# Block transposes on VectorE with a trip through DRAM in place of TensorE's transposes, in a fused attention and two-MLP kernel

## The chip, the cores and the metric
The program runs on one core of a Trainium2 chip, in one launch. The metric is the device time of that core in microseconds. A core has five engines with a queue each: TensorE (PE in the profile; its weight loads are PEld), VectorE (DVE), ScalarE (ACT), GpSimd (POOL) and SyncE (SP). An engine works through its own queue in order; semaphores make it wait for others. All transfers of this kernel but the instruction fetches are issued on SP's queue.

## The reference
Sliding-window attention (4 batches, 8 heads, 576 positions, head size 64, window 64), whose output is reshaped to 2304 tokens of 512 and goes through two MLPs:

```
scores = scale * q @ k.T ; mask 0 <= i - j < 64 ; softmax ; @ v        # per head
h = x @ w_in (512 -> 2048) ; g = h * tanh(softplus(h)) ; x2 = g @ w_out (2048 -> 512)
h = x2 @ w_in2 (512 -> 1024) ; solu = h * softmax(h)
ln = (solu - mean) / sqrt(var + 1e-6) * g_ln ; out = ln @ w_out2 (1024 -> 512)
```

## The kernel before, in words
Matmuls run in a 32-bit form with each operand split in a high and a low part (`hi`, `lo`), three products per pair of operands where both are split.

**Attention.** The tokens come in 36 blocks of 64 queries. The first four blocks are done singly, the other 32 in 16 pairs n = 4, 6, ... 34 (`attend`). A pair goes: scores into PSUM (`a_qk`), from pair 8 on scaling and mask on VectorE into an SBUF tile `s` (`a_scale`), maximum, subtraction, exponential, sum, reciprocal, multiplication, then eight 128x128 transposes on TensorE into PSUM (`a_tr`, L837), two copies back to SBUF on ScalarE (`a_pt`), and the second product with v (`a_pv`, L874), whose result is split into the token tile `xt` of its group. There are five groups of tokens (512, 512, 512, 384, 384).

**First MLP.** 84 items (`mish`), each a group of tokens by 128 of the 2048 hidden units: first layer (`pe_m1`, L920, 12 matmuls), activation on ScalarE, split, second layer (`pe_m2`, L954, 8 matmuls, `pe_m2l`, L965, 4) into four PSUM accumulators, evicted and stored to DRAM (`x2d`).

**Second MLP.** 18 tiles of 128 tokens, two at a time (u = 0 to 8). Two tiles are loaded, combined to sums, split; seven products of half-size blocks (`b_p`, L1089, six matmuls each) go to four PSUM banks, are evicted and added on VectorE (`b_c`). Per tile: maximum, exponential, product and moments, normalisation in place in tile `h_b` (`b_z`, L1165), eight 128x128 transposes on TensorE into PSUM (`b_tr`, L1172), split by ScalarE (`b_hi`, L1178) and VectorE (`b_lo`, L1182), output matmuls (`b_m4`, L1197, three groups of eight), eviction on ScalarE (`b_out`, L1204) and store (L1208).

**What sets the order.** A planner (`Schedule`) walks all steps, with a cost per engine and buffer rings of given sizes, and issues the step that can start first by its costs; among near ones the table `RANK`, one number per step, decides. What each engine runs, and in which order, is thus fixed before the program runs. Waits come from data and buffers. Where the planner sees TensorE idle, it fills in matmuls on zeros (`bridge`, L687).

Of the kernel before, what the change touches and what calls it, by code (L numbers as in the profile page):

```python
# [1615 lines left out]
```

## Time and profile before

| | us |
|---|---|
| device time, median of 3 runs | 684.72 (683.97 to 684.91) |
| the profiled execution | 684.38 |
| its span | 682.5 |
| TensorE busy | 672.4 (99%) |
| VectorE busy | 393.7 (58%) |
| ScalarE busy | 346.5 (51%) |
| GpSimd busy | 37.4 (5%) |

The span runs from the first to the last instruction; the execution's own time holds a little more. Busy times count the time in which an engine runs something. The chain of waits follows back from the last instruction, at each step to what released it or to the instruction ahead of it on its engine, and so says what a shorter piece would be worth.

### The profile page before, as it was taken

What the parts mean: (1) busy time and instruction counts of PE and PEld (TensorE: products, weight loads), DVE (VectorE), ACT (ScalarE), POOL (GpSimd) and SP (SyncE); (2) the same over time, 40 slices, a digit from 0 to 9 for tenths busy, and PEclk for the clock granted to TensorE, in tenths of its full rate; (3) what the DMA queues carried; (4) which work ended last, traced back from release to release, by engine and by line L of the source; (5) the groups of instructions that cost most, each with busy time, mean ns of one, the idle gap of its engine ahead of it and who ended that gap; (6) DMA issues with size and microseconds to landing.
All of it is one profiled execution on the core that took longest, in us unless ns stands there. A gap on an engine that the chain in (4) does not pass through costs nothing.

```text
span 682.5 us, 10711 instructions
## 1 busy us (share of the span) xinstructions
PE 672.4 (99%) x4326; PEld 581.2 (85%) x4326; DVE 393.7 (58%) x693; ACT 346.5 (51%) x623; POOL 37.4 (5%) x63
## 2 busy tenths in 40 slices
PE   8899999999999999999999999999999999999997
PEld 6788888888888888888899999999888888888886
DVE  4887887775676143111116637747686678484461
ACT  6889965443357243112223545547665455564352
POOL 3212100000001000000001000000010001000010
PEclk9999999999999999999999999999999999999999
DMA  9886575563355020000043235103310111010001
GB/s 325 323 278 215 164 242 161 179 215 123 120 179 198 0 92 33 0 1 0 11 145 124 63 124 181 52 27 98 109 42 36 63 47 46 32 48 31 16 31 47
DMA packets 36801, 72.00 MB, mean 105 GB/s; under 512 B 2832, under 2 KB 14096, under 8 KB 36752
## 3 DMA queue, kind: packets, MB, share of 16 engines
q1 hardware_dynamic: 36752, 71.32, 31.0%
q8 instruction: 34, 0.56, 0.3%
q14 instruction: 15, 0.12, 0.1%
HBM read 59.77 MB, written 11.53 MB: 104 GB/s over the span
## 4 chain that ended last, share of the span: by engine, by line
PE 95%; DMA 2%; ACT 1%; issue 0%; DVE 0%; SPq 0%; ACTq 0%
PE ps_h L920 29%; PE x L954 19%; PE po L1197 14%; PE pb L1089 13%; PE x L965 10%; PE ps_o L874 2%; PE ps_s L735 2%; PE pt L1172 2%; PE ps_t L837 2%; DMA st<-w_out 1%; DMA qk<-qk 1%; PE ps_s L717 0%; ACT st L473 0%; PE ps_h L687 0%; ACT L930 0%
## 5 line engine op out<-in xcount | busy, mean ns | idle before, releaser
L920 PE MATMUL ps_h<-xt,w 128*128 128x512 f32 (+2 forms) x1008 | 205.3, 360 | 0.2 <-ACT mc L930 0.2
L920 PEld LDWEIGHTS ps_h<-xt,w 128*128 128x128 f32 x1008 | 177.0, 188 | 21.8 <-ACT mc L930 0.6
L954 PE MATMUL x<-g,w 128*128 128x512 f32 (+2 forms) x672 | 146.9, 360 | 0.5 <-DVE g L409 0.5
L954 PEld LDWEIGHTS x<-g,w 128*128 128x128 f32 x672 | 118.4, 188 | 14.9 <-DVE g L409 0.8
L425 DVE SCALAR_TENSOR_TENSOR g<-mc,g 128x512 fp32r<-128x512 f32 (+2 forms) x84 | 51.0, 613 | 94.5 <-ACT g L405 93.8
L1197 PE MATMUL po<-w,lz 128*128 128x512 f32 x432 | 102.4, 391 | 0.0
L930 ACT ACTIVATE mc<-ps_h 128x512 f32<-128x512 f32 (+2 forms) x84 | 44.4, 535 | 99.7 <-PE ps_h L920 84.7
L1197 PEld LDWEIGHTS po<-w,lz 128*128 128x128 f32 x432 | 80.7, 188 | 16.8
L965 PE MATMUL x<-g,w 128*128 128x512 f32 (+2 forms) x336 | 80.5, 361 | 0.0
L965 PEld LDWEIGHTS x<-g,w 128*128 128x128 f32 x336 | 59.6, 188 | 7.2 <-issue 0.7
L405 ACT ACTIVATE g<-mc 128x512 fp32r<-128x512 f32 (+2 forms) x59 | 33.8, 575 | 61.7 <-PE x L965 60.9
L1089 PE MATMUL pb<-w,xs 128*128 128x512 f32 x210 | 52.2, 398 | 0.0
L1089 PEld LDWEIGHTS pb<-w,xs 128*128 128x128 f32 x210 | 38.9, 188 | 8.7
L1182 DVE TENSOR_TENSOR lz<-pt,lz 128x512 fp32r<-128x512 f32 x36 | 24.0, 687 | 30.7 <-ACT lz L1178 30.6
L1089 PE MATMUL pb<-w,xs_w 128*128 128x512 f32 x168 | 40.8, 393 | 0.0
L1089 PEld LDWEIGHTS pb<-w,xs_w 128*128 128x128 f32 x168 | 31.2, 188 | 6.4
L409 DVE CAST g<-mc 128x512 fp32r<-128x512 f32 (+2 forms) x25 | 9.9, 395 | 43.4 <-PE x L965 41.3
L825 POOL TENSOR_TENSOR s<-s,rs 128x1024 f32<-128x1024 f32 x7 | 15.1, 2157 | 337.5 <-DVE rs L819 336.2
L490 DVE SCALAR_TENSOR_TENSOR st<-st 128x1024 uint32<-128x1024 uint32 x22 | 27.4, 1248 | 8.8 <-ACT st L482 6.2
L417 ACT ACTIVATE s<-ps_t 128x512 f32<-128x512 f32 x32 | 18.1, 596 | 25.3 <-PE ps_t L837 25.3
L1204 ACT ACTIVATE o<-po 128x512 f32<-128x512 f32 x18 | 10.8, 599 | 38.5 <-PE po L1197 37.7
L482 ACT ACTIVATE st<-st 128x1024 uint32<-128x1024 uint32 x22 | 25.1, 1147 | 9.8 <-DMA st<-w_in 4.2
(138 smaller groups left out, 757.1 us busy)
## 6 DMA issues: line engine op xcount, KB each, us to landing
qk<-qk SPq DMA_DIRECT2D x32, 512.0 KB, 5.2
st<-w_out SPq DMA_DIRECT2D x12, 1024.0 KB, 5.1
st<-w_in SPq DMA_DIRECT2D x10, 1024.0 KB, 5.9
v<-v SPq DMA_DIRECT2D x32, 256.0 KB, 3.8
xr<-x2d SPq DMA_DIRECT2D x18, 256.0 KB, 3.3
out<-o SPq DMA_DIRECT2D x18, 256.0 KB, 2.0
x2d<-xs SPq DMA_DIRECT2D x12, 256.0 KB, 2.7
part<-xs SPq DMA_DIRECT2D x8, 256.0 KB, 4.8
```

What stands on the lines that cost most here:

```text
L405: nc.scalar.activation(out=hi, in_=x, func=ACTF.Copy, scale=1.0 if g is None else g)
L417: nc.scalar.activation(out=out, in_=x, func=ACTF.Copy)
L425: nc.vector.scalar_tensor_tensor(out=lo, in0=x, scalar=1.0 if g is None else g, in1=hi.bitcast(F32), op0=ALU.mult, op1=ALU.subtract)
L482: nc.scalar.activation(out=w, in_=w, func=ACTF.Copy, scale=0.9325 * 2.0**-29)
L490: nc.vector.scalar_tensor_tensor(out=lw, in0=uw, scalar=3, in1=lw, op0=ALU.logical_shift_left, op1=ALU.bitwise_or)
L920: nc.tensor.matmul(out=ps[:, :n], lhsT=w[:, a, k, fs], rhs=x[:, b, k, a0:a1], start=(idx == 0), stop=(idx == len(terms) - 1),)
L930: nc.scalar.activation(out=c[:, :n], in_=ht.pop(i)[:, :n], func=ACTF.Mish)
L954: nc.tensor.matmul(out=acc[j][m][:, a0:a1], lhsT=w[:, a, f % 4, m * P:(m + 1) * P], rhs=g[:, 0, :n], start=(i in opens and a == 0), stop=F ...
L965: nc.tensor.matmul(out=acc[j][m][:, a0:a1], lhsT=w[:, 0, f % 4, m * P:(m + 1) * P], rhs=g[:, 1, :n], start=False, stop=i in closes,)
L1089: nc.tensor.matmul(out=ps, lhsT=x[:, a, ix, k, :], rhs=w[:, k, :], start=first and n == 0, stop=n == len(terms) - 1, skip_group_check=not ...
L1182: nc.vector.tensor_tensor(out=lt[t][:, 1, fs], in0=pst[t][:, fs], in1=lt[t][:, 0, fs].bitcast(F32), op=ALU.subtract)
L1197: nc.tensor.matmul(out=po[t], lhsT=lz[:, a, f, :], rhs=wt["w4", f // 4][:, b, f % 4, :], start=(c == 0 and idx == 0), stop=(c == 2 and idx ...
```

## The change
The transposes of the pairs n >= 16 (ten pairs) and of all 18 tiles of the second MLP leave TensorE. For those pairs the score tile `s` is laid out in four column blocks of 32, so that scaling is four instructions; one VectorE instruction (`nc.vector.transpose`) transposes each 32x32 block, one DMA writes the tile to DRAM (`blocks_out`, 512 KB) and four DMAs read it back (`blocks_in`, 128 KB each, to 32 partitions, in pieces of 1 KB), which puts the blocks in their places. In the second MLP it is the same, from `h_b` into a tile `y_b`, and back into `h_b`, which the split then reads. The ring of `h_b` grows from 4 to 6; the PSUM pool for the transposes goes. The warm-up at the start has 16 matmuls of one kind instead of 13 of another and 5 of it. `RANK` holds new numbers, so the order changes everywhere. The diff, cut to its core:

```
+N_T = 16
+SPLIT = "p f (i c) -> p i f c"
...
+    def blocks_out(key, src):
+        d = blocks[key] = dram.tile([4, 32, 4, 256], F32, tag="t_d", name="t_d", bufs=4)
+        nc.sync.dma_start(out=d.rearrange("i a b x -> (i a) b x"), in_=src.rearrange("p b h c -> p b (h c)"))
+
+    def blocks_in(key, dst):
+        d = blocks.pop(key)
+        for b in range(4):
+            r = slice(32 * b, 32 * b + 32)
+            nc.sync.dma_start(out=dst[r].rearrange("a i h c -> a i (h c)"), in_=d[:, :, b].rearrange("i a x -> a i x"))
...
-        z = m_p.tile([P, 2, GMAX], F32R, tag="g", name="warm_r", bufs=LAG)
...
-        zeros(a, 5)
+        zeros(ps_h.tile([P, 512], F32, tag="h", name="ps_w"), N_WARM)
...
+            s = at_p.tile([P, 4, 2 * NP, 32], F32, tag="s2", name="s", bufs=2)
+            for b in range(4):
+                k = slice(32 * b, 32 * b + 32)
+                mb = m[:, k].unsqueeze(1).to_broadcast([P, 2 * NP, 32])
+                nc.vector.scalar_tensor_tensor(out=s[:, b], in0=ps[:, :, k], scalar=scale, in1=mb, op0=ALU.mult, op1=ALU.add)
...
+    def a_blocks(n):
+        nc.vector.transpose(out=s_t[n], in_=s_t[n])
+
+    def a_out(n):
+        blocks_out(n, s_t.pop(n))
+        pt_t[n] = at_p.tile([P, 4, 2 * NP, 32], F32, tag="s2", name="pt", bufs=2)
+
+    def a_in(n):
+        blocks_in(n, pt_t[n])
...
-                        rhs=pt[:, p, r] if n < N0 else pt[:, h * NP + p, a:a + BLK],
+                        rhs=pt[:, p, r] if n < N0 else pt[:, h * NP + p, a:a + BLK] if n < N_T
+                        else pt[:, a // 32:a // 32 + 2, h * NP + p, :],
...
-                hs[t] = B["z"].tile([P, 2, 512], F32, tag="h", name="h_b", bufs=4)
+                hs[t] = B["z"].tile([P, 2, 512], F32, tag="h", name="h_b", bufs=6)
...
-            for f in range(NF2):
-                nc.tensor.transpose(pst[t][:, f, :], z[:, f // 4, (f % 4) * P:(f % 4 + 1) * P], ident)
+            y = B["z"].tile([P, 4, NF2, 32], F32, tag="ty", name="y_b")
+            nc.vector.transpose(out=y, in_=z.rearrange("p h f -> p (h f)").rearrange("p (f b a) -> p b f a", f=NF2, b=4))
+            pst[t] = y, z
+
+        def b_out_t(t):
+            blocks_out(("z", t), pst[t][0])
+
+        def b_in_t(t):
+            z = pst[t][1]
+            pst[t] = z.rearrange("p h f -> p (h f)").rearrange("p (i f c) -> p i f c", i=4, f=NF2)
+            blocks_in(("z", t), pst[t])
...
-            nc.scalar.activation(out=lt[t][:, 0, fs], in_=pst[t][:, fs], func=ACTF.Copy)
+            nc.scalar.activation(out=lt[t][:, 0, fs].rearrange(SPLIT, i=4), in_=pst[t][:, :, fs], func=ACTF.Copy)
```

TensorE at the end of the program, before: `pb` are the banks of the seven products, `pt` the transposes, `po` the output accumulators of one tile each, `lz` the split tiles.

```order
L1172 MATMUL pt_5881<-ident_70,h_b_5717 128x128 x8
L1089 MATMUL pb_5892<-w33_3945,xs_4240 128x512 x6
L1197 MATMUL po_5911<-w40_4251,lz_5901 128x512 x8
L1089 MATMUL pb_5816<-w32_4148,xs_4240 128x512 x6
L1172 MATMUL pt_5936<-ident_70,h_b_5823 128x128 x8
L1197 MATMUL po_5911<-w41_4165,lz_5901 128x512 x8
L1197 MATMUL po_5911<-w40_4251,lz_5901 128x512 x4
L1197 MATMUL po_5911<-w41_4165,lz_5901 128x512 x4
L1197 MATMUL po_5983<-w40_4251,lz_5959 128x512 x8
L1197 MATMUL po_5983<-w41_4165,lz_5959 128x512 x8
L1172 MATMUL pt_6012<-ident_70,h_b_5842 128x128 x8
L1197 MATMUL po_5983<-w40_4251,lz_5959 128x512 x4
```

And now, from the last products on (L1118 is the line of the products, L1235 that of the output matmuls):

```order
L1118 MATMUL pb_5761<-w33_4000,xs_4193 128x512 x6
L1235 MATMUL po_5729<-w41_4116,lz_5516 128x512 x8
L1235 MATMUL po_5729<-w40_4228,lz_5516 128x512 x4
L1235 MATMUL po_5729<-w41_4116,lz_5516 128x512 x4
L1118 MATMUL pb_5672<-w32_4158,xs_4193 128x512 x6
L1235 MATMUL po_5822<-w40_4228,lz_5817 128x512 x8
L1235 MATMUL po_5822<-w41_4116,lz_5817 128x512 x8
L1235 MATMUL po_5822<-w40_4228,lz_5817 128x512 x4
L1235 MATMUL po_5822<-w41_4116,lz_5817 128x512 x4
L1235 MATMUL po_5876<-w40_4228,lz_5845 128x512 x8
```

Before, the last product (`pb_5816`) stood ahead of most of tile 14's output matmuls, and a set of transposes stood ahead of each tile's. Now no transposes stand there, and the last product (`pb_5672`) is followed by the output matmuls of six tiles (12 to 17) and nothing else.

SP's queue in the same place, before: loads of token tiles (`xr`) and stores of the output (`out`).

```order
L1041 DMA xr_5221<-x2d3_66 128x4x128
L1208 DMA out<-o_5239 128x512
L1041 DMA xr_5221<-x2d4_67 128x4x128
L1208 DMA out<-o_5311 128x512
L1208 DMA out<-o_5411 128x512
```

And now, in the same stretch and at the end (`t_d` is the tile in DRAM; L375 is the write, L381 the reads):

```order
L1070 DMA xr_5424<-x2d4_67 128x4x128
L375 DMA t_d_5449<-y_b_5426 128x1024
L381 DMA h_b_5132<-t_d_5449 32x4x256 x4
L1246 DMA out<-o_5499 128x512
L375 DMA t_d_5559<-y_b_5540 128x1024
L1246 DMA out<-o_5562 128x512
L381 DMA h_b_5339<-t_d_5559 32x4x256 x4
L375 DMA t_d_5664<-y_b_5636 128x1024
L381 DMA h_b_5331<-t_d_5664 32x4x256 x4
L1246 DMA out<-o_5716 128x512
```

Each tile adds a write and four reads to SP's queue, and the reads stand right behind their write, with at most a store or a load between.

## Rows read from the trace of the kernel before

**Rows 1.** The page: busy time by engine, and the chain that ended last.
```profile
PE 672.4 (99%) x4326; PEld 581.2 (85%) x4326; DVE 393.7 (58%) x693; ACT 346.5 (51%) x623; POOL 37.4 (5%) x63
...
PE 95%; DMA 2%; ACT 1%; issue 0%; DVE 0%; SPq 0%; ACTq 0%
```

**Rows 2.** Stretches: length, busy time by engine, granted clock, DMA share, GB/s.
```profile
0.00:36.00 36.00, 30.65 (x388) 25.18 (x389) 23.93 (x48) 27.23 (x89) 9.36 (x21) 1.00 0.87 312
36.00:100.00 64.00, 63.38 (x570) 55.87 (x570) 53.61 (x70) 56.09 (x125) 9.40 (x4) 1.00 0.67 228
100.00:345.00 245.00, 245.00 (x1499) 203.91 (x1498) 111.48 (x141) 93.87 (x131) 1.90 (x1) 1.00 0.30 98
345.00:475.00 130.00, 129.55 (x905) 127.15 (x905) 74.24 (x104) 62.20 (x96) 1.90 (x1) 1.00 0.30 98
475.00:682.50 207.50, 203.84 (x969) 169.09 (x967) 130.39 (x333) 107.14 (x185) 14.79 (x36) 1.00 0.14 45
```

**Rows 3.** The chain in order of time, transposes: start, length, what.
```profile
157.83 0.87 PE ps_t L837 x8
...
394.18 0.87 PE ps_t L837 x8
...
501.03 0.87 PE pt L1172 x8
...
670.69 0.87 PE pt L1172 x8
```

**Rows 4.** Groups of instructions by form: busy us, mean ns.
```profile
L409 DVE CAST w<-st 128x1024 fp32r<-128x1024 f32 x11 | 7.6, 688 | 0.3
...
L802 DVE TENSOR_TENSOR s<-s,nm 128x1024 f32<-128x1024 f32 x10 | 13.1, 1305 | 0.3
...
L825 POOL TENSOR_TENSOR s<-s,rs 128x1024 f32<-128x1024 f32 x7 | 15.1, 2157 | 337.5 <-DVE rs L819 336.2 <-ACT room_b L473 1.3
...
L788 DVE SCALAR_TENSOR_TENSOR s<-ps_s,mask_n 128x1024 f32<-128x1024 f32 x11 | 13.4, 1215 | 3.9 <-PE ps_s L735 3.8
...
L425 DVE SCALAR_TENSOR_TENSOR xs<-xr,xs 128x256 fp32r<-128x256 f32 x5 | 2.1, 418 | 0.0
```

**Rows 5.** Transfers: KB, median us to landing; time of issue on SP (ns).
```profile
out<-o SPq DMA_DIRECT2D x18, 256.0 KB, 2.0
...
xr<-x2d SPq DMA_DIRECT2D x14, 256.0 KB, 3.2
...
qk<-qk SPq DMA_DIRECT2D x18, 512.0 KB, 4.7
...
xs<-part SPq DMA_DIRECT2D x8, 256.0 KB, 6.4
...
L1208 SPq DMA_DIRECT2D out<-o x18: 332/333/344, 510.6 to 679.6; - x18
...
L1041 SPq DMA_DIRECT2D xr<-x2d x18: 518/530/1599, 456.9 to 598.2; - x18
```

**Rows 6.** The chain in order of time, matmul groups: start, length, what.
```profile
306.26 2.72 PE ps_h L920 x12
...
654.78 1.40 PE pb L1089 x6
...
657.05 7.30 PE po L1197 x32
664.36 0.87 PE pt L1172 x8
```

**Rows 7.** The timeline: start, length, instruction, count and idle time ahead.
```profile
4.10 1.29 PE L687 MATMUL ps_w<-warm 128*128 128x256 bf16 x5
...
661.82 0.80 DVE L1165 TENSOR_SCALAR h_b<-h_b,st,c 128x1024 f32<-128x1024 f32 x1
...
665.27 1.09 ACT L1178 ACTIVATE lz<-pt 128x512 fp32r<-128x512 f32 x2 [2.29 <-PE pt L1172]
...
666.99 0.80 DVE L1165 TENSOR_SCALAR h_b<-h_b,st,c 128x1024 f32<-128x1024 f32 x1
```

More of the change, by code (lines that the diff above doesn't have):

```diff
@@ L363, in attention_moe_solu @@
     g_sb = const.tile([P, NF2], F32, name="g_sb")
+    blocks = {}
+    def blocks_out(key, src):
[6 more added lines that the diff above has]
+            nc.sync.dma_start(out=dst[r].rearrange("a i h c -> a i (h c)"), in_=d[:, :, b].rearrange("i a x -> a i x"))
     def keep(m, op, base, k, q):
@@ L669, in warm_up @@
         room["warm"] = w
-        z = m_p.tile([P, 2, GMAX], F32R, tag="g", name="warm_r", bufs=LAG)
-        nc.vector.memset(z[:, 0, :256].bitcast(F32), 0.0)
-        z = z[:, 0, :256]
-        a, b = (ps_h.tile([P, 512], F32, tag="h", name="ps_w") for _ in range(2))
-        for _ in range(4):
-            nc.tensor.matmul(out=a[:, :256], lhsT=z[:, :P], rhs=z, start=True, stop=True)
-        for _ in range(3):
-            for h, o in ((0, a), (1, b)):
-                r = slice(h * BLK, (h + 1) * BLK)
-                nc.tensor.matmul(out=o[:, :256], lhsT=z[r, :P], rhs=z[r], start=True, stop=True)
-        for _ in range(3):
-            nc.tensor.matmul(out=a[:BLK, :256], lhsT=z[:, :BLK], rhs=z, start=True, stop=True)
-        zeros(a, 5)
+        zeros(ps_h.tile([P, 512], F32, tag="h", name="ps_w"), N_WARM)
     def zeros(ps, n):
@@ L778, in a_exp1 @@
             nc.scalar.activation(
-                out=s[:, p], in_=s[:, p], func=ACTF.Exp, bias=nm[:, p:p + 1], accum_out=su[:, p:p + 1]
+                out=by_head(n, s)[0][:, p], in_=by_head(n, s)[0][:, p], func=ACTF.Exp, bias=nm[:, p:p + 1],
+                accum_out=su[:, p:p + 1],
             )
@@ L784, in a_scale, with by_head @@
         ps = s_t[n]
-        s = at_p.tile([P, 2 * NP, P], F32, tag="s2", name="s", bufs=2)
         m = mask_0 if any(i % NBB == 0 for i in (n, n + 1)) else mask_n
-        m = m.unsqueeze(1).to_broadcast([P, 2 * NP, P])
-        nc.vector.scalar_tensor_tensor(out=s, in0=ps, scalar=scale, in1=m, op0=ALU.mult, op1=ALU.add)
+        if n < N_T:
+            s = at_p.tile([P, 2 * NP, P], F32, tag="s2", name="s", bufs=2)
+            m = m.unsqueeze(1).to_broadcast([P, 2 * NP, P])
+            nc.vector.scalar_tensor_tensor(out=s, in0=ps, scalar=scale, in1=m, op0=ALU.mult, op1=ALU.add)
+        else:
+            s = at_p.tile([P, 4, 2 * NP, 32], F32, tag="s2", name="s", bufs=2)
[3 more added lines that the diff above has]
+                nc.vector.scalar_tensor_tensor(out=s[:, b], in0=ps[:, :, k], scalar=scale, in1=mb, op0=ALU.mult, op1=ALU.add)
         s_t[n] = s
+    def by_head(n, s):
+        return (s, AX.X) if n < N_T else (s.rearrange("p b h a -> p h b a"), AX.XY)
     def a_max(n):
@@ L793, in a_max @@
         nm = sm_p.tile([P, 2 * NP], F32, tag="nm2", name="nm")
-        nc.vector.tensor_reduce(out=nm, in_=s, axis=AX.X, op=ALU.max, negate=True)
+        x, axis = by_head(n, s)
+        nc.vector.tensor_reduce(out=nm, in_=x, axis=axis, op=ALU.max, negate=True)
         if n < NM:
@@ L800, in a_sub @@
         s, nm = s_t[n]
-        nm = nm.unsqueeze(2).to_broadcast([P, 2 * NP, P])
+        nm = nm.unsqueeze(2).to_broadcast([P, 2 * NP, P]) if n < N_T else nm.unsqueeze(1).unsqueeze(3).to_broadcast(list(s.shape))
         nc.vector.tensor_tensor(out=s, in0=s, in1=nm, op=ALU.add)
@@ L810, in a_sum @@
         su = sm_p.tile([P, 2 * NP], F32, tag="su2", name="su")
-        nc.vector.tensor_reduce(out=su, in_=s, axis=AX.X, op=ALU.add)
+        x, axis = by_head(n, s)
+        nc.vector.tensor_reduce(out=su, in_=x, axis=axis, op=ALU.add)
         s_t[n] = s, None, su
@@ L824, in a_mul @@
         eng = nc.gpsimd if e == "pool" else nc.vector
-        eng.tensor_tensor(out=s, in0=s, in1=rs.to_broadcast(list(s.shape)), op=ALU.mult)
+        eng.tensor_tensor(out=s, in0=s, in1=(rs if n < N_T else rs.unsqueeze(1)).to_broadcast(list(s.shape)), op=ALU.mult)
         s_t[n] = s
@@ L1029, in open_b2 @@
             B["z"] = ctx.enter_context(tc.tile_pool(name="bz", bufs=2, reuse_waits="tile"))
-            B["t"] = ctx.enter_context(tc.tile_pool(name="pb_t", bufs=1, space=PSUM, reuse_waits="tile"))
             B["o"] = ctx.enter_context(tc.tile_pool(name="pb_o", bufs=2, space=PSUM, reuse_waits="tile"))
@@ L1169, in b_tr @@
             z = zt.pop(t)
-            pst[t] = B["t"].tile([P, NF2, P], F32, tag="t", name="pt")
-            for f in range(NF2):
-                nc.tensor.transpose(pst[t][:, f, :], z[:, f // 4, (f % 4) * P:(f % 4 + 1) * P], ident)
+            y = B["z"].tile([P, 4, NF2, 32], F32, tag="ty", name="y_b")
[7 more added lines that the diff above has]
+            blocks_in(("z", t), pst[t])
         def b_hi(t, c):
@@ L1182, in b_lo @@
             nc.vector.tensor_tensor(
-                out=lt[t][:, 1, fs], in0=pst[t][:, fs], in1=lt[t][:, 0, fs].bitcast(F32), op=ALU.subtract
+                out=lt[t][:, 1, fs].rearrange(SPLIT, i=4), in0=pst[t][:, :, fs],
+                in1=lt[t][:, 0, fs].bitcast(F32).rearrange(SPLIT, i=4), op=ALU.subtract
             )
@@ L1305, in attention_moe_solu @@
             convert(p)
-        warm, warm2, warm3 = Buf("h"), Buf("h"), Buf("g")
-        step(dict(pe=0.107 * N_WARM), -200, warm_up, new=[warm, warm2, warm3], uses=[warm, warm2, warm3])
+        warm = Buf("h")
+        step(dict(pe=0.107 * N_WARM), -200, warm_up, new=[warm], uses=[warm])
         x_of, x_first, x_all, xbuf, pv_of, pv_last = {}, {}, {}, {}, {}, []
@@ L1351, in attend_first @@
             finish(n, t, offs[8:], mu, ([room_kv, room_s], s), O, [cp])
+        moved = []
         def attend(n, t, offs, gate):
@@ L1367, in attend @@
                 qk = step(dict(pe=0.88), t + offs[0], a_qk, n, after=lks + pv_of_old, new=[S], uses=ks + [S], mode="qk")
-                sc = step(dict(dve=1.23), t + offs[1], a_scale, n, after=[qk, masks, mask_x], new=[s], uses=[S, s])
+                sc = step(dict(dve=1.23 if n < N_T else 1.55), t + offs[1], a_scale, n, after=[qk, masks, mask_x] + moved[-1:], new=[s], uses=[S, s])
                 mx = step(dict(dve=1.2), t + offs[2], a_max, n, after=[sc], new=[nm], uses=[s, nm])
@@ L1382, in attend @@
             mu = step(COSTS["mul"], t + offs[6], a_mul, n, after=[r], uses=[s, rs], two=True)
-            tr = step(dict(pe=0.87), t + offs[7], a_tr, n, after=[mu] + pv_last[-1:], new=[T], uses=[s, T])
-            c0 = step(COSTS["pt"], t + offs[8], a_pt, n, 0, after=[tr], uses=[T, s])
-            c1 = step(COSTS["pt"], t + offs[8], a_pt, n, 1, after=[tr, c0], uses=[T, s])
-            finish(n, t, offs[9:], mu, (ws, s), O, [c0, c1])
+            if n < N_T:
+                tr = step(dict(pe=0.87), t + offs[7], a_tr, n, after=[mu] + pv_last[-1:], new=[T], uses=[s, T])
+                c0 = step(COSTS["pt"], t + offs[8], a_pt, n, 0, after=[tr], uses=[T, s])
+                c1 = step(COSTS["pt"], t + offs[8], a_pt, n, 1, after=[tr, c0], uses=[T, s])
+                c = [c0, c1]
+            else:
+                T = Buf("s2")
+                bl = step(dict(dve=1.13), t + offs[7], a_blocks, n, after=[mu], uses=[s])
+                td = Buf("td")
+                mo = step(dict(dma=1.4), t + offs[8], a_out, n, after=[bl], new=[td, T], uses=[s, td])
+                c0 = step(dict(dma=2.0), t + offs[8], a_in, n, after=[mo], uses=[T, td])
+                moved.append(mo)
+                c, s = [c0, c0], T
+            finish(n, t, offs[9:], mu, (ws, s), O, c)
             pv_of[n].after += lvs
@@ L1549, in attention_moe_solu @@
             z = step(dict(dve=0.82), o[3], b_z, t, after=[sh], uses=[h, st])
-            T, lz = Buf("bt"), Buf("blz")
-            tr = step(dict(pe=0.87), o[4], b_tr, t, after=[z, ob2], new=[T], uses=[h, T])
-            h0 = step(dict(act=0.478), o[5], b_hi, t, 0, after=[tr], new=[lz], uses=[T, lz])
-            l0 = step(dict(dve=0.602), o[5], b_lo, t, 0, after=[h0], uses=[T, lz])
-            h1 = step(dict(act=0.478), o[5], b_hi, t, 1, after=[h0], uses=[T, lz])
-            l1 = step(dict(dve=0.602), o[5], b_lo, t, 1, after=[h1], uses=[T, lz])
+            Y, lz = Buf("bty"), Buf("blz")
+            tr = step(dict(dve=1.13), o[4], b_tr, t, after=[z, ob2], new=[Y], uses=[h, Y])
+            td = Buf("td")
+            mo = step(dict(dma=1.4), o[4], b_out_t, t, after=[tr], new=[td], uses=[Y, td])
+            mv = step(dict(dma=2.0), o[4], b_in_t, t, after=[mo], uses=[h, td])
+            h0 = step(dict(act=0.55), o[5], b_hi, t, 0, after=[mv], new=[lz], uses=[h, lz])
+            l0 = step(dict(dve=0.69), o[5], b_lo, t, 0, after=[h0], uses=[h, lz], two=True)
+            h1 = step(dict(act=0.55), o[5], b_hi, t, 1, after=[h0], uses=[h, lz])
+            l1 = step(dict(dve=0.69), o[5], b_lo, t, 1, after=[h1], uses=[h, lz], two=True)
             O, ot = Buf("bo"), Buf("bot")
@@ L1564, in attention_moe_solu @@
             w1=4, w2=4, st=2, e=2, qk=LD, v=LD, a=1, s=N_S, nm=4, rs=4, s2=2, nm2=4, rs2=4, x2=4, h=2, xt=2, mc=2,
-            g=LAG, xs=4, bxr=1, bxs=1, bsum=1, bk0=1, bk1=1, bk2=1, bk3=1, bh=4, bnm=4, bsu=4, by=2, bst=4, bt=1, blz=2, bo=2, bot=2,
+            g=LAG, xs=4, bxr=1, bxs=1, bsum=1, bk0=1, bk1=1, bk2=1, bk3=1, bh=6, bty=2, td=4, bnm=4, bsu=4, by=2, bst=4, blz=2, bo=2, bot=2,
         ))
```

158 rows, old and new, of the table RANK are left out of this document.

## The prediction, made before the changed kernel ran

> **What bounds the kernel now.** I read the busy shares first: TensorE is busy 672.4 of 682.5 us, and the chain that ended last is 95% TensorE [rows 1]. Then the stretches [rows 2]: after the first 36 us, where transfers run at 312 GB/s and TensorE idles 5.4 us, it stands still for 0.6 us up to 100 us, not at all up to 345 us, and for 0.5 us up to 475 us. In the second MLP (from about 475 us) only the last 3.7 us lack it, which are the last eviction, the store and the end. [...] So an instruction taken off TensorE is worth its slot in the chain, if nothing new makes TensorE wait; VectorE has 77 us idle in the second MLP (130.4 busy of 207.5) and 190 us between 100 and 475 us [rows 2].
>
> **What goes.** The chain of waits has each set of eight transposes as a piece of its own: 0.87 us, in ten pairs (first at 157.83, last at 394.18 us) and in 18 tiles of the second MLP (first at 501.03, last at 670.69) [rows 3]. One of the ten stands there with 1.02; the gaps around them are nil, the next piece begins where the set ends. 28 x 0.87 = 24.4 us. That is the whole first-order gain, 15.7 in the second MLP and 8.7 in the pairs. ScalarE loses two copies out of PSUM per pair; it is busy 93.9 of 245 us there [rows 2], so I give nothing for that.
>
> **What comes, VectorE.** One transpose instruction of 128x1024 per pair and per tile. No row shows one. The nearest rows of that shape: a cast at 0.688 us, a subtraction at 1.305 us, and far off, on GpSimd, a multiply at 2.157 us [rows 4]. A block transpose reads and writes each element once like the subtraction, whose two operands it lacks; I take 1.15 us, ends 0.69 and 2.16. In the second MLP VectorE gets 18 x 1.15 = 20.7, together 151.1 us in 207.5 - 15.7 = 191.8 us, 79%. In the 36 to 100 us stretch the same engine was busy 53.6 of 64 us, 84%, while TensorE lost 0.6 us [rows 2]: 79% can be carried. At 2.16 it would be 169.3 us, 88%, above what any stretch here shows.
> [...]
> The scaling of a pair becomes four instructions of 256 elements at 0.418 each [rows 4] for one at 1.215: 0.46 us more, ten times, beside 190 us of idle VectorE. The split of the second MLP's tiles keeps its element counts and reads SBUF where it read PSUM; ScalarE, busy 107.1 of 207.5 us [rows 2], hides what that may cost.
>
> **What comes, transfers.** Per pair and tile one write of 512 KB to DRAM and four reads of 128 KB in pieces of 1 KB, all on SP's queue, the reads behind the landing of the write. Write: 256 KB land in 2.0 us (the output stores) and 512 KB loads took 4.7 in the busier middle [rows 5]; I take 3.0 (ends 2.0 and 4.7). Reads: 256 KB in pieces of 512 B land in 3.2 us, loads behind one another in 6.4; issuing costs SP 0.33 for a store of 128 rows [rows 5], so the fourth read goes 1.0 us behind the first: I take 4.5 (ends 3.2 and 6.4 + 1.0). With 0.5 us of hand-overs the round trip is 8 us, ends 5.2 and 12.6. What was one PE set of 0.87 us between the normalised tile and ScalarE's split becomes 1.15 + 8 = 9.2 us of latency.
> [...]
>
> **The cover of that latency.** It is TensorE work that stands between a tile's last product and its output matmuls. At the end of the program, where it must be thinnest, the last product ends at 656.18 us (654.78 + 1.40), and the tiles 16 and 17 are normalised at 662.62 and 667.79 us [rows 6, 7]: 6.4 and 11.6 us later. Add 9.2, and 0.55 for the first split [rows 7]: 16.2 and 21.4 us. In the new order the last product is followed by all output matmuls of the tiles 12 to 15 before those of 16: 12 groups of eight at 7.30 / 4 = 1.825 us [rows 6], 21.9 us, and 27.4 before tile 17. Spare: 5.7 and 6.0 us; the round trip may be half as long again. Before, the order gave tile 16's transposes 8.2 us. Earlier the cover is larger: before the first output matmuls stand 17 products (at 1.40, [rows 6]) behind tile 1's last, 23.8 us, later two tiles' products and four to six tiles' matmuls.
> In the pairs the ring of score tiles (two buffers) now holds scores and result of one pair, so a pair's reads wait for the second product of the pair before. The thinnest stretch between two such products holds three groups of the first layer, 3 x 2.72 = 8.2 us [rows 6], against 4.5 for the reads, 7.4 at their upper end.
>
> **The start.** The warm-up turns from 13 + 5 into 16 matmuls of the second kind, 1.29 / 5 = 0.26 us each [rows 7], 4.1 us from about 1.2 us on: it ends where it ended. The order of the first loads differs but holds the same bytes, and the stretch is ruled by transfers. I put 0, plus or minus 2.
>
> **Sum.** The profiled execution took 684.38 us, 682.5 of it span; the median of the runs is 684.72, 0.3 above, so no correction. 684.4 - 24.4 = 660.0. For thin places (a pair, the first tiles, VectorE at 79%) I add 2.0, about twice what TensorE lost between 36 and 475 us before: **662.0 us**.
>
> **Rivals.**
> (1) Part of the gain comes back as waits for transfers. VectorE's second split stands in its queue and waits for the reads, and everything behind it waits too. VectorE has (191.8 - 151.1) / 18 = 2.3 us of idle per tile; what a tile blocks it beyond that, TensorE loses. With the round trip at its upper end, 4.6 us longer, the spare of 5.7 at the end is nearly gone, and if 3 us of it block VectorE in each tile, 18 x 0.7 = 12.6 are lost: 675 us. For: SP is one queue, and its longest waits grow. Against: the orders leave 20 us and more.
> (2) VectorE becomes the bound, its transpose at the upper end of 2.16 us. 169.3 us of work at 84% busy take 201.5 instead of 191.8 us: 662 + 10 = 672 us. For: it is a new instruction. Against: the cast and the subtraction of the same shape on the same engine.
> (3) Slower than before: SP's queue sets the pace of the second MLP. In it each write's landing L is waited for before the reads are issued, and loads and stores stand behind. A tile takes SP 0.35 + L + 4 x 0.33 + 0.53 (load) + 0.33 (store) [rows 5] = 2.5 + L. It is slower from 207.5 / 18 + 8.7 / 18 = 12.0 us per tile on, so from L = 9.5. At 10.5 the stage is 13.0 x 18 = 234, and the time 684.4 - 8.7 + 26.5 = 702 us. For: nothing but a write followed by reads of the same place, which no row shows back to back. Against: the longest median landing is 6.4 us, in a stretch with twice the 45 GB/s of this one [rows 2, 5].
>
> **Chances.** Forecast (657 to 667 us) 0.74; (1), 667 to 682, 0.14; (2) 0.06; (3) 0.04; another way to no gain 0.02. The range takes the forecast's own width, (2) and the nearer half of (1): 657 to 676. A measurement can tell 0.2% (1.4 us) from no change: faster 0.92 (the forecast, (2), and (1) but for 0.02), same 0.02, slower 0.06 ((3) and the rest of (1)).
>
> **What would show it.** Right: no transposes of the second MLP and 80 fewer of the pairs in TensorE's rows; TensorE's busy time near 648 us, still 98% of the span; a VectorE transpose near 1.15 us; the write landing in about 3 us, the reads in 4 to 5; VectorE near 80% from 475 us on. Wrong: TensorE waiting for ScalarE's split of the output matmuls by more than a microsecond in many tiles (1), VectorE above 88% with TensorE waiting for its sums (2), or SP's longest waits being on its own writes while products wait for their loads (3). A gap before a pair's second product would name the ring of score tiles.

## The result, and the profile after

| | time, median (range, runs) | ratio to before, 95% interval |
|---|---|---|
| before | 684.35 us (683.73 to 684.91, 4) | |
| after | 667.19 us (665.53 to 668.40, 4) | 0.975 [0.972, 0.977] |

17.2 us came off where 22.4 were forecast. The profiled execution took 667.13 us, 665.4 of it span. The page's busy times, and the chain that ended last by engine:

```profile
PE 649.1 (98%) x4089; PEld 556.8 (84%) x4089; DVE 423.6 (64%) x741; ACT 348.3 (52%) x616; POOL 40.9 (6%) x63
...
PE 77%; DMA 10%; DVE 6%; ACT 3%; SPq 2%; issue 1%; POOL 0%; ACTq 0%; DVEq 0%
```

TensorE lost 23.3 us of work against [rows 1], and the span 17.1. The chain, 95% TensorE before, now runs through transfers, VectorE and ScalarE for a fifth of the span. The stretches, with the columns of [rows 2]; the fourth ends at 455 us because the second MLP now begins earlier:

```profile
0.00:36.00 36.00, 30.38 (x359) 24.88 (x359) 23.49 (x46) 28.31 (x89) 10.88 (x22) 1.00 0.88 322
36.00:100.00 64.00, 62.19 (x581) 54.40 (x580) 53.17 (x71) 52.44 (x119) 5.69 (x3) 1.00 0.62 206
100.00:345.00 245.00, 242.85 (x1463) 201.47 (x1462) 121.80 (x167) 95.14 (x128) 2.03 (x1) 1.00 0.42 138
345.00:455.00 110.00, 109.61 (x781) 107.32 (x780) 69.06 (x97) 54.77 (x79) 1.92 (x1) 1.00 0.36 118
455.00:665.40 210.40, 204.03 (x912) 168.75 (x910) 156.05 (x363) 117.61 (x202) 20.34 (x36) 1.00 0.46 142
```

From 100 to 345 us TensorE stands still for 2.15 us where it had no gap, and in the last stretch for 6.4 where the last stretch of before lacked 3.7. VectorE is at 156.05 / 210.4 = 74% there. The transfers, 45 GB/s in the second MLP before, are at 142. The new work, by form (busy us, mean ns) and by transfer (KB, median us to landing):

```profile
L1200 DVE STREAM_TRANSPOSE y_b<-h_b 128x1024 f32<-128x1024 f32 x18 | 22.2, 1236 | 0.0
...
L861 DVE STREAM_TRANSPOSE s<-s 128x1024 f32<-128x1024 f32 x10 | 12.4, 1243 | 2.0 <-POOL s L844 1.8
...
t_d<-y_b SPq DMA_DIRECT2D x18, 512.0 KB, 2.8
h_b<-t_d SPq DMA_DIRECT2D x72, 128.0 KB, 3.2
...
t_d<-s SPq DMA_DIRECT2D x10, 512.0 KB, 3.3
pt<-t_d SPq DMA_DIRECT2D x40, 128.0 KB, 3.1
```

The transpose costs 1.24 us, the write lands in 2.8 to 3.3, each read in 3.1 to 3.2. TensorE's waits by line and releaser, those behind 100 us that are new:

```profile
PE po L1235 <- ACT lz L1215: 2.5, 2, 1.7
PE ps_o L903 <- DMA pt<-t_d: 2.1, 2, 1.9
```

Two pairs and two tiles; none of the other 24 shows one. Of the larger wait in the pairs, the timeline (start, length, instruction, count, idle time ahead and its releaser):

```profile
233.13 0.80 SPq L643 DMA_DIRECT2D qk<-qk  x2
...
235.72 0.33 SPq L375 DMA_DIRECT2D t_d<-s  x1
...
241.53 1.75 SPq L381 DMA_DIRECT2D pt<-t_d  x4
...
241.64 1.42 DVE L802 SCALAR_TENSOR_TENSOR s<-ps_s,mask 128x256 f32<-128x256 f32 x4 [5.94 <-DMA t_d<-s]
...
246.09 1.15 PE L903 MATMUL ps_o<-pt,v 128*64 128x64 f32 x32 [1.89 <-DMA pt<-t_d]
```

SP issued two loads of 512 KB, then the write. The reads, which need the landed write, went 5.8 us behind it, while the median landing is 3.3. And the larger wait of the second MLP, before its first output matmuls:

```profile
482.18 9.71 PE L1118 MATMUL pb<-w,xs_w 128*128 128x512 f32 x42
...
495.44 0.81 DVE L1194 TENSOR_SCALAR h_b<-h_b,st,c 128x1024 f32<-128x1024 f32 x1
...
496.77 1.24 DVE L1200 STREAM_TRANSPOSE y_b<-h_b 128x1024 f32<-128x1024 f32 x1
...
498.04 2.30 SPq L375 DMA_DIRECT2D t_d<-y_b  x2
...
500.91 1.80 SPq L381 DMA_DIRECT2D h_b<-t_d  x4
...
506.80 1.15 ACT L1215 ACTIVATE lz<-h_b 128x512 fp32r<-128x512 f32 x2 [1.66 <-DMA h_b<-t_d]
...
507.48 4.68 PE L1235 MATMUL po<-w,lz 128*128 128x512 f32 x18 [1.67 <-ACT lz L1215]
```

The products of the first two tiles end where those of the next two begin, at 482.2 us. The first tile is normalised 14 us later, and from there transpose, write, reads and first split follow one behind the other to 507.48.

### The profile page after: what moved, and what is told of

Same layout as the page of the kernel before. It is cut to its first block, busy times and chain, and to the rows that moved or that the text cites. A ratio compares the mean times of both kernels' runs of the same rounds, so it can differ in the third digit from the quotient of the medians.

```text
span 665.4 us, 10569 instructions
## 1 busy us (share of the span) xinstructions
PE 649.1 (98%) x4089; PEld 556.8 (84%) x4089; DVE 423.6 (64%) x741; ACT 348.3 (52%) x616; POOL 40.9 (6%) x63
## 4 chain that ended last, share of the span: by engine, by line
PE 77%; DMA 10%; DVE 6%; ACT 3%; SPq 2%; issue 1%; POOL 0%; ACTq 0%; DVEq 0%
PE ps_h L950 26%; PE x L984 18%; PE po L1235 10%; PE x L995 9%; PE pb L1118 9%; DMA t_d<-s 3%; PE ps_o L903 2%; PE ps_s L741 2%; DMA h_b<-t_d 2%; DMA t_d<-y_b 2%; DMA st<-w_in 1%; SPq L381 1%; DMA room_q<-qk 1%; DMA pt<-t_d 1%; DMA xr<-x2d 1%
## 5 line engine op out<-in xcount | busy, mean ns | idle before, releaser
L1235 PE MATMUL po<-w,lz 128*128 128x512 f32 x432 | 101.4, 391 | 2.6 <-ACT lz L1215 2.5
L1235 PEld LDWEIGHTS po<-w,lz 128*128 128x128 f32 x432 | 80.6, 188 | 21.4 <-ACT lz L1215 4.6
L423 ACT ACTIVATE g<-mc 128x512 fp32r<-128x512 f32 (+2 forms) x68 | 39.2, 578 | 60.4 <-PE x L995 59.3
L1118 PE MATMUL pb<-w,xs 128*128 128x512 f32 x210 | 51.1, 395 | 0.0
L1118 PEld LDWEIGHTS pb<-w,xs 128*128 128x128 f32 x210 | 39.4, 188 | 9.2
L1118 PE MATMUL pb<-w,xs_w 128*128 128x512 f32 x168 | 39.8, 390 | 0.0
L1118 PEld LDWEIGHTS pb<-w,xs_w 128*128 128x128 f32 x168 | 31.5, 188 | 6.7
L1215 ACT ACTIVATE lz<-h_b 128x512 fp32r<-128x512 f32 x36 | 21.3, 626 | 29.6 <-DMA h_b<-t_d 19.4
L1219 DVE TENSOR_TENSOR lz<-h_b,lz 128x512 fp32r<-128x512 f32 x36 | 24.0, 686 | 17.3 <-ACT lz L1215 17.2
L844 POOL TENSOR_TENSOR s<-s,rs 128x1024 f32<-128x1024 f32 x6 | 11.5, 1923 | 354.0 <-DMA x2d<-xs 187.3
L435 ACT ACTIVATE v_b<-pb 128x512 f32<-128x512 f32 x33 | 19.6, 595 | 20.0 <-PE pb L1118 18.2
L1150 ACT ACTIVATE e<-h_b,nm 128x1024 f32<-128x1024 f32 x18 | 20.7, 1151 | 9.1 <-DVE nm L1141 8.9
```

What stands on the lines that cost most here:

```text
L423: nc.scalar.activation(out=hi, in_=x, func=ACTF.Copy, scale=1.0 if g is None else g)
L1118: nc.tensor.matmul(out=ps, lhsT=x[:, a, ix, k, :], rhs=w[:, k, :], start=first and n == 0, stop=n == len(terms) - 1, skip_group_check=not ...
L1215: nc.scalar.activation(out=lt[t][:, 0, fs].rearrange(SPLIT, i=4), in_=pst[t][:, :, fs], func=ACTF.Copy)
L1219: nc.vector.tensor_tensor(out=lt[t][:, 1, fs].rearrange(SPLIT, i=4), in0=pst[t][:, :, fs], in1=lt[t][:, 0, fs].bitcast(F32).rearrange(SPLI ...
L1235: nc.tensor.matmul(out=po[t], lhsT=lz[:, a, f, :], rhs=wt["w4", f // 4][:, b, f % 4, :], start=(c == 0 and idx == 0), stop=(c == 2 and idx ...
```

## The experiments

Ratios are against the kernel before on the same chip, whose median was 684.88, 684.96 and 684.74 us in the three series.

### What the trip costs: after without it

`e1_no_trip`. The planned order stays; the ring of `y_b` has 4 tiles, not 2.

```diff
         # a_out, a_in
-        blocks_out(n, s_t.pop(n))
-        pt_t[n] = at_p.tile([P, 4, 2 * NP, 32], F32, tag="s2", name="pt", bufs=2)
+        pt_t[n] = s_t.pop(n)
-        blocks_in(n, pt_t[n])
         # b_out_t, b_in_t
-            blocks_out(("z", t), pst[t][0])
...
-            blocks_in(("z", t), pst[t])
+            pst[t] = pst[t][0]
```

> The changed kernel without the trip through DRAM: the block transposes stay on VectorE, but their results are used where they stand, so all 28 writes and 112 reads are gone and the blocks are not put in their places; the order of every engine is kept. Theory (latency of the trip is what ate the gain): the four waits of TensorE that follow a read (0.26 at 213, 1.89 at 246, 1.67 at 507, 0.87 at 567 us, together 4.7) go, the others (1.7 us between 36 and 100 us) stay: 667.2 - 4.7 = 662.5 us, TensorE idle 11.5 us. Rival (VectorE's added work, or the new order by itself): 666 to 668 us.

661.53 us (661.18 to 661.85), ratio 0.966 [0.965, 0.967]. The trip, latency and traffic together, costs 667.19 - 661.53 = 5.7 us; the two intervals leave some 2 us either way. TensorE's waits at the four places account for 4.7 of it (0.26, 1.89, 1.67 and 0.87), and its matmuls ran 1.4 us longer in after (649.1 us busy for 647.7). The stretches of this run from 100 to 345 and from 455 us, with the columns as above:

```profile
100.00:345.00 245.00, 245.00 (x1476) 203.71 (x1475) 121.78 (x167) 94.96 (x128) 2.16 (x1) 1.00 0.32 108
...
455.00:659.50 204.50, 200.84 (x898) 166.75 (x896) 153.44 (x359) 115.34 (x201) 20.33 (x36) 1.00 0.16 53
```

All four waits are gone, with VectorE's transposes in place: TensorE has no gap from 100 to 345 us, and the last stretch lacks 3.7 as before.

### What the block transposes cost: after without them

`e2_no_blocks`.

```diff
-        nc.vector.transpose(out=s_t[n], in_=s_t[n])
+        pass
...
-            y = B["z"].tile([P, 4, NF2, 32], F32, tag="ty", name="y_b")
-            nc.vector.transpose(out=y, in_=...)
-            pst[t] = y, z
+            pst[t] = z.rearrange(...), z
```

> The changed kernel without VectorE's 28 block transposes (the tiles make the trip untransposed), the rest and the order kept. VectorE is relieved of 18 x 1.236 + 10 x 1.243 = 34.7 us, and each trip starts 1.24 us earlier. Theory (latency): the waits shrink by at most 1.24 each, 0.26 + 1.24 + 1.24 + 0.87 = 3.6: 663.6 to 666 us, and the one at 246 us stays in part, because its write lands late for another reason. Rival (VectorE's work): all of the missing time comes back, 660 to 662 us, and TensorE waits nowhere behind a sum or a product of VectorE.

664.94 us (663.47 to 668.80), ratio 0.972 [0.969, 0.974]. The 2.2 us less are within what 1.24 us less of latency give, and the range is wide. In the profile, which is of the longest run (668.8 us), TensorE's waits for the splits fall from 2.5 to 0.2 us; those in the pairs, where a write lands late, do not shrink. That VectorE's time itself is the price falls with the run above, where all 28 transposes stay and the time is 661.5.

### What the removed transposes were worth: before without them

`e3_before_no_tr`. The 28 sets are left out of the kernel before, the scores and the normalised tile are used as they lie (ring of `h_b` 6, as in after).

```diff
+            if n >= 16:
+                pt_t[n] = s, s
+                return
...
-            for f in range(NF2):
-                nc.tensor.transpose(pst[t][:, f, :], z[:, f // 4, ...], ident)
+            pst[t] = z.rearrange("p h f -> p (h f)").rearrange("p (f c) -> p f c", f=NF2)
```

> The kernel before without the 28 sets of eight transposes on TensorE that the change removes (ten pairs, 18 tiles): their readers take the untransposed tile from SBUF, and the ring of tiles in the second MLP has 6 places as in the changed kernel; order and all else kept. It shows what the sets are worth when nothing replaces them. Theory: 0.87 us each, 684.4 - 24.4 = 660.0 us. Rival (TensorE's slot was in part cover for others, which now wait): 663 to 667 us, with the lost time as new waits of TensorE.

661.43 us (661.25 to 662.15), ratio 0.966 [0.965, 0.967]: 23.45 us for 28 sets, 0.84 each. It is the same time as after without its trip (661.53), so the transposes on VectorE, the four-part scaling, the shorter warm-up and the new order together cost about 0.1 us.

### The ring of score tiles: reading back in place

`e4_in_place`. A pair's reads go into its own score tile; nothing waits for the second product of the pair before.

```diff
-        blocks_out(n, s_t.pop(n))
-        pt_t[n] = at_p.tile([P, 4, 2 * NP, 32], F32, tag="s2", name="pt", bufs=2)
+        pt_t[n] = s_t.pop(n)
+        blocks_out(n, pt_t[n])
```

> The changed kernel, but the ten pairs read their blocks back into the score tile itself, as the second MLP does, and so hold one of the ring's two tiles instead of both; the order is kept. A pair's scaling need not wait for the landing of the write of the pair before (VectorE's 14.7 us of such waits go). Theory (the 1.89 us at 246 us is that chain): this wait and the one at 213 us go, 667.2 - 2.1 = 665.1 us. Rival (the write lands late at 241 us because two loads of 512 KB were issued just ahead of it): the wait stays, 667 us.

667.02 us (665.53 to 668.10), no change. VectorE no longer waits for the write, but the reads of the pair near 236 us still go only at 240.48, 4.65 us behind their write. TensorE's waits at the two pairs are 1.14 and 0.73 us in this profile, together 1.9 for 2.15. So it was the landing of the write and not the ring.

### The share of the pairs

`e10_pairs_no_trip`: the pairs' half of the first edit alone.

```diff
-        blocks_out(n, s_t.pop(n))
-        pt_t[n] = at_p.tile([P, 4, 2 * NP, 32], F32, tag="s2", name="pt", bufs=2)
+        pt_t[n] = s_t.pop(n)
...
-        blocks_in(n, pt_t[n])
```

> Leaves out the write and the four reads of the ten pairs alone: the block transposes are used where they stand, so the rest of each block is not put in place; the second MLP keeps its trip. The trip as a whole costs 5.7 us (667.2 against 661.5). Theory: what it costs is the sum of TensorE's waits that the trace shows, 2.2 us in the pairs (0.26 and 1.89) and 2.5 in the second MLP: 664.7 us, 664 to 665.3, with the waits near 213 and 246 us gone and the two of the second MLP kept. Rival: the 5.7 us lie in the second MLP, where the trip's traffic is densest, and the pairs' waits are made up for later: 666.5 to 667.5.

664.61 us (662.86 to 666.90), ratio 0.971 [0.969, 0.973]. 667.19 - 664.61 = 2.6 us for the ten pairs, 664.61 - 661.53 = 3.1 for the 18 tiles; TensorE's waits in the profile of after were 2.15 and 2.5. The intervals leave some 2 us either way on each part, so the split is a rough one. The waits near 505 and 564 us stay. Put together, 684.9 - 23.45 + 0.1 + 2.6 + 3.1 = 667.2; each term is a difference between two of these runs, so the sum must come out and proves nothing further. What supports it is that the waits, read from the trace, are near these sizes.

### The late write: another queue

`e7_pair_pool`.

```diff
+        q = nc.gpsimd if isinstance(key, int) else nc.sync
-        nc.sync.dma_start(out=d..., in_=src...)
+        q.dma_start(out=d..., in_=src...)
```

> The write of the ten pairs is issued on GpSimd's queue and no longer on SP's; reads and everything else stay. Theory: the write of the pair near 236 us lands late (5.8 us against a median of 3.3) because it stands behind two loads of 512 KB in SP's queue. On a queue of its own it lands in 3.3 us, the reads of that pair go 2 to 3 us earlier, TensorE's waits near 213 and 246 us are gone: 664.7 us (664 to 665.5). Rival: the loads and the write share the same 16 engines, so the write lands late from any queue: the wait of 1 to 2 us near 246 stays and the time with it, 666.5 to 668.

668.86 us (667.00 to 669.78), ratio 0.977 [0.975, 0.978]: a little above the rival's range, and the theory falls. The pair of above, in this run's timeline:

```profile
234.12 0.80 SPq L644 DMA_DIRECT2D qk<-qk  x2
...
236.97 0.53 POOL L376 DMA_DIRECT2D t_d<-s  x1 [15.78 <-DVE s L862]
...
241.66 1.75 SPq L382 DMA_DIRECT2D pt<-t_d  x4
...
246.42 1.15 PE L904 MATMUL ps_o<-pt,v 128*64 128x64 f32 x32 [1.24 <-DMA pt<-t_d]
```

Issued on another queue, the write still takes 4.7 us here and 6.8 near 203 us (5.0 in after), and the waits stay. What delays it is not its place in SP's queue.

`e8_all_act`: all 28 writes.

```diff
-        nc.sync.dma_start(out=d..., in_=src...)
+        nc.scalar.dma_start(out=d..., in_=src...)
```

> All 28 writes are issued on ScalarE's queue. Theory: as with the pairs' writes on another queue, the waits in the pairs go; in the second MLP SP no longer stands at a write until VectorE's transpose is done, so the loads behind it go earlier, and the waits near 507 and 567 us shrink by the 0.3 us of the issue each: 664 to 666. Rival: ScalarE now stands at each write until VectorE's transpose is done (1.24 us and what is ahead of it), its exponentials and first splits behind it come late, and TensorE gets new waits for ScalarE in the second MLP: 669 to 674.

674.03 us (672.97 to 675.39), ratio 0.985 [0.983, 0.986]: the rival's range. The late pair is as late as before (write at 238.09, reads at 243.53 us), and in the second MLP ScalarE issues the second tile's write only at 504.27:

```profile
500.52 0.33 ACTq L375 DMA_DIRECT2D t_d<-y_b  x1
...
504.21 0.60 ACT L435 ACTIVATE v_b<-pb 128x512 f32<-128x512 f32 x1 [1.56 <-PE pb L1118]
504.27 0.33 ACTq L375 DMA_DIRECT2D t_d<-y_b  x1
```

ScalarE came to it behind a copy that waited for TensorE. On SP both writes were out by 500.34. TensorE's wait before the first output matmul is 2.94 us in this run, for 1.67.

### The late write: ahead of the loads

`e11_write_first`. Loads of queries and keys that come between a pair's scaling and its write are issued behind the write, or at the first product that needs them.

```diff
+        if s.fn.__name__ == "a_scale" and s.args[0] >= N_T:
+            self.behind = []
+        if s.fn.__name__ == "load_qk" and self.behind is not None:
+            self.behind.append(s)
+            return
...
+        if s.fn.__name__ == "a_out":
+            for x in self.behind or ():
+                x.fn(*x.args)
+            self.behind = None
```

> The two loads of queries and keys of a later pair that SP issued just ahead of a pair's write are issued right behind it; the result and all other orders stay. Theory: the write lands late (5.1 us near 203, 5.8 near 236) because the 16 DMA engines still work on the 1 MB ahead of it, whichever queue issues it, as the runs with the write on two other queues showed. With the write ahead it lands in about 3 us, the reads go 2 us earlier even if they share the engines with those loads, and the waits of TensorE near 213 and 246 us go: 664.6 us (664.0 to 665.5), as without the trip in the pairs. Rival: the loads now stand ahead of the reads and these land late instead: the wait near 246 stays above 1 us and the time at 666.5 to 668.

676.23 us (674.45 to 676.73), ratio 0.987 [0.986, 0.988]. Both missed, by an oversight in the edit: it also held back two loads until the product that needs them was due, near 150 us, and TensorE waited 4.1 us for them. The products that started at 144.14 us in after are 1.5 us late in this run, ahead of that wait, and those that started at 159.07 are 8.0 us late. So the wait and what came of it cost 6.5 of the 9.0 us. At the places it was made for:

```profile
244.88 0.33 SPq L388 DMA_DIRECT2D t_d<-s  x1
...
245.30 1.21 SPq L656 DMA_DIRECT2D qk<-qk  x2
...
247.89 1.75 SPq L394 DMA_DIRECT2D pt<-t_d  x4
...
254.24 1.15 PE L916 MATMUL ps_o<-pt,v 128*64 128x64 f32 x32 [0.88 <-DMA pt<-t_d]
```

The write lands in 3.0 us instead of 5.8, as the theory had it. The reads now follow the loads and land late, as the rival had it: a pair's read takes 4.6 us in the median for 3.1. The wait here shrank from 1.89 to 0.88 us, and the one near 213 grew from 0.26 to 1.41. In these rows, what was put ahead was paid by what was put behind: 2.8 us less for this write, 1.5 us more for a pair's read in the median. Two loads just ahead do not always make a write late: the one at 362.64 us in after stood as closely behind two such loads and landed in 3.4 us. What made the difference is not shown.

### A longer trip

`e5_hop`. The hop, too, is issued on SP's queue, so SP also stands at it until the write has landed (28 waits of SP, 90.0 us together).

```diff
-        nc.sync.dma_start(out=d..., in_=src...)
+        e = dram.tile([4, 32, 4, 256], F32, tag="t_e", name="t_e", bufs=4)
+        nc.sync.dma_start(out=e..., in_=src...)
+        nc.sync.dma_start(out=d..., in_=e...)
```

> Each of the 28 trips gets one more hop of 512 KB, from DRAM to DRAM, between its write and its reads: some 3 us more of latency (by the write's 2.8 to 3.3), the same result. Theory: the order covers the trip with little to spare, so each place that waits now waits about 3 us more (four places, 12 us) and some of the other 24 begin to wait, while SP stands at the hop as well: 680 us, 675 to 688. Rival: the cover was as large as forecast (5.7 us at the end, 3.7 in the pairs), and only the two longest waits grow: 670 to 673.

750.10 us (747.34 to 750.72), ratio 1.095 [1.093, 1.097]: both far too low. The hop lands in 4.0 us (median of 28), and the time grows by 83 us, 3.0 for each of 28 trips. The first products of the second MLP start 23 us later than in after (486.91 for 464.04); the other 60 are lost behind that. A stretch of the chain that ended last (start, length, what):

```profile
599.32 0.53 ACT lz L1217
599.88 0.69 DVE lz L1221
600.57 0.72 DVE h_b L1196
601.31 0.69 DVE h_b L1135
602.01 1.16 DVE y_b L1202
603.19 2.62 DMA t_e<-y_b
605.83 4.52 DMA t_d<-t_e
610.37 0.33 SPq L383
...
611.69 3.09 DMA h_b<-t_d
...
614.88 0.64 ACT lz L1217
```

One tile's splits (`lz`) wait for its reads. Behind them in VectorE's queue stand the next tile's normalisation and transpose, and its write, hop and reads begin only then: two trips that should overlap run one after the other. The same chain goes on, and there it is another queue:

```profile
620.16 4.02 DMA t_d<-t_e
624.20 0.30 SPq L383
...
626.02 3.57 DMA t_e<-y_b
```

The next tile had been transposed by 622.7 us, but its write stood in SP's queue behind the reads of the tile before, and these waited for the landing of their hop. Of the 18 writes of the second MLP, eight were issued at once behind their transpose and ten 1.9 to 7.9 us behind it, 50 us together; in after it was three, 3.6 us together. So both queues, VectorE's and SP's, made the trips serial, and no run separates their shares. Of the 83 us some 25 are matmuls that ran longer (TensorE busy 673.8 us for 649.1), at a mean granted clock of 0.956; the rest is idle time.

`e12_hop_planned`: the same, and the planner counts 1.5 us more behind the write of a second-MLP tile.

```diff
+LATE = dict(b_out_t=1.5)
...
-            t = max([d.end + delay(d.engine, e) for d in s.after], default=-9.0)
+            t = max([d.end + delay(d.engine, e) + LATE.get(d.fn.__name__, 0.0) for d in s.after], default=-9.0)
```

> The run with one more hop of 512 KB (750.1 us), where the planner now counts 1.5 of the hop's 4.4 us in the second MLP and nothing in the pairs. Theory: the hop costs so much (83 us) because an order made for a shorter trip makes two tiles' trips serial: the second split waits in VectorE's queue with the next tile's transpose behind it. An order made for part of it gets part back: 715 to 735 us. Rival: the loop of write, hop, reads, splits and next transpose sets the pace in any order that these rings allow: 745 to 755.

732.17 us (726.92 to 735.74), ratio 1.069 [1.065, 1.073]: 18 us of the 83 come back by order alone, as the theory had it. No run has a larger allowance, so how far this goes stays open.

### A later order for after

`e13_plan_1_0` and `e14_plan_1_5`: on top of `e11_write_first`, with its wait at 155 us, 1.0 and 1.5 us more for the reads of a tile.

```diff
+LATE = dict(b_in_t=1.0)
...
-            t = max([d.end + delay(d.engine, e) for d in s.after], default=-9.0)
+            t = max([d.end + delay(d.engine, e) + LATE.get(d.fn.__name__, 0.0) for d in s.after], default=-9.0)
```

> As the last, and the planner counts 1.0 us more for the reads of a tile of the second MLP, so that it orders the work for a longer trip. The first output matmuls then come about one group of six products (1.4 us) later. Theory: the two waits of TensorE in the second MLP, 1.7 near 507 and 0.9 near 567, are places where the order allows less than the trip takes; they go, and the time is 662.0 to 663.5, near the 661.5 without any trip. Rival: the later order only moves the waits to other tiles: 664 to 666, as the run before.

> The same with 1.5 us. Theory: no wait is left to take away beyond the run with 1.0, so the time is the same within 1 us, 662 to 663.5. Rival: each half microsecond more keeps taking away waits that one profile does not show, and it is another 1 us lower, or the end of the program, where the last tile's trip then has less behind it, gets longer by 1 to 2 us: 664 to 665.

680.32 us (679.04 to 680.82) and 682.74 (681.74 to 686.61), 4.1 and 6.5 us above the run they build on. The wait before the first output matmuls falls from 2.21 to 0.18 us with 1.0, as expected, but the waits behind it grow: in the second MLP they add up to 4.8 us for 3.7, with 2.07 at 667 us the longest. Most of the rest of the loss lies in matmuls that ran longer (TensorE busy 654.1 us for 651.8). With 1.5 there is

```profile
657.11 23.98 PE L1251 MATMUL po<-w,lz 128*128 128x512 f32 x96 [7.72 <-ACT lz L1231]
```

in the profile of its longest run (span 684.8 us): the order has nothing left to put under the trips of the last four tiles. No kernel with the reference's full work beat after by more than the runs can tell.

## Why the prediction was right or wrong

The result lies just above the forecast's own 657 to 667 us, in the band of the first rival (667 to 682). It is inside the stated range, 657 to 676, because that took in the nearer half of this rival. And what the first rival said, that part of the gain comes back as waits for transfers, is what happened, in a small measure.

**What goes** held: 23.45 us by the run without the sets, for 24.4.

**VectorE** held. 1.24 us for 1.15; 74% busy for 79%. The second rival (VectorE the bound, 672) falls with the run without the trip.

**The lengths of the transfers** held in the median. Write 2.8 and 3.3 for 3.0; the reads 3 x 0.43 of issue and 3.2 of landing make 4.5, as forecast. By tile, the trace has 4.3 to 7.2 us from the first read's issue to the last landing, 4.8 in the median. No median here is near the upper end of 7.4; the reads of one tile were, the second one's (7.2 us), which overlapped with those of the first.

**The cover** is the step that failed, at two places. "Earlier the cover is larger: before the first output matmuls stand 17 products behind tile 1's last, 23.8 us" was true of the products: from 482.2 us they last to 505.8. But the 6.4 us from the last product to the first normalised tile were taken from the end of the program. At the stage's beginning they are 14.1 (482.18 to 495.44 + 0.81). With the forecast trip of 9.2 and the split of 0.55 that makes 23.8 us, the whole cover. The trace of before had nearly as long a time at this place. There the products of the first two tiles end at 487.12, and the first tile is normalised 12.2 us later (timeline of before):

```profile
487.12 9.71 PE L1089 MATMUL pb<-w,xs_w 128*128 128x512 f32 x42
...
498.51 0.81 DVE L1165 TENSOR_SCALAR h_b<-h_b,st,c 128x1024 f32<-128x1024 f32 x1
```

With 12.2 in place of 6.4, the prediction's own sum would have left a spare of 1.9 us here. Two stretches of after around the place:

```profile
480.00:497.00 17.00, 17.00 (x76) 13.87 (x75) 13.35 (x40) 12.73 (x22) 2.44 (x4) 1.00 0.11 32
497.00:508.00 11.00, 9.33 (x41) 7.26 (x40) 10.25 (x24) 5.95 (x11) 0.00 (x0) 1.00 0.82 206
```

VectorE is busy 13.35 and ScalarE 12.73 of 17 us while the first tile waits for its statistics, and VectorE 10.25 of 11 us during the trip. The transfers then run at 206 GB/s, not at the 45 of the stage before [rows 2], since the trips themselves are the traffic (10 of the 12 transfers issued there, 2.0 of 2.5 MB): from the first read's issue to the first split it took 5.9 us, for 4.5. So the first tile had no spare. The last ones had theirs: no wait of TensorE for a split comes after 567 us.

In the pairs the thinnest stretch was right (8.3 us between two second products, from 283.40 to 291.71, and no wait there), but the prediction counted only the reads against it. The late landing of the write (5.8 us) was the length that decided. "A gap before a pair's second product would name the ring of score tiles" was wrong: the gap came, and the ring was not its cause.

**The sum.** The term "2.0 for thin places" was mis-sized; it measured 5.7. 662.0 + 3.7, and 1.0 for the smaller worth of the sets, make 666.7 of the 667.19 measured. The start, put at 0, idled 5.6 us for 5.4; between 36 and 100 us it was 1.8 for 0.6, which the run without the trip has too (1.6).

**The rivals.** The first named a mechanism (the second split stands in VectorE's queue and what stands behind it waits), and after has little of it: one tile makes TensorE wait for its split by more than a microsecond. The run with the hop shows it in full, and shows that its price was far too low: 675 us for a trip that is 4.6 us longer, where a hop of 4.0 us made 750. The spare of 5.7 us at the end was no reserve either, because the trips no longer overlapped. The third rival had SP's queue, which waits for each landing, set the pace. The run with the hop shows this too, in the ten writes that stood behind the tile before. Its sum does not fit: it put the turn to slower at a landing of 9.5 us, and with write and hop at some 8 us the kernel is already 65 us slower than before.

## What to carry to other kernels

Count the latency that an order must cover from the moment the tile is really ready, at the fill of the stage and with the traffic that the change itself brings, and not from the drain at its end. A trip of 8 us that is hidden in 24 of 28 places may have no reserve: look on every in-order queue, the one that issues the transfers too, for what stands behind the instruction that waits for the data, since one longer step there can turn overlapped trips into serial ones (here a hop of 4.0 us in each of the 28 trips cost 83). Another queue or another order among the transfers may only move the lateness, as it did here (from GpSimd's queue the two late writes took 6.8 and 4.7 us for 5.0 and 5.8; with the write ahead a pair's read took 4.6 for 3.1); measure a version without the transfer first, to know what can be won at all (here 5.7 us).
